# Row-stacked queries for the exact chunks: scores that contract over 64 rows instead of 128 rows with zeros

## The chip, the cores and the metric

The kernel runs on one core of one Trainium2 chip. Its engines are TensorE (PE for its matmuls, PEld for the weight loads that go with them), VectorE (DVE), ScalarE (ACT), GpSimd (POOL) and SyncE (SP, which here only issues transfers). The metric is the device time of one execution in microseconds, the median of three runs.

## The reference, cut to what matters

Two stages are computed, one behind the other. The first is attention over 4 batches, 8 heads, 768 positions and a head size of 64, in which a query sees the first `n_sink` = 4 keys and the `window` = 128 keys up to its own position:

```python
scores = scale * np.matmul(q, k.transpose(0, 1, 3, 2))      # scale = 1 / sqrt(64)
keep = is_sink | in_window
scores = np.where(keep, scores, -1000000000.0)
scores = scores - np.max(scores, axis=-1, keepdims=True)
a = np.exp(scores)
a = a / (np.sum(a, axis=-1, keepdims=True) + 1e-09)
attn_out = np.matmul(a, v).astype(np.float32)
```

The second takes the 3072 rows of that output, 512 wide, through a feed-forward layer of width 2048 with a softplus:

```python
h = x @ w_in
g = np.maximum(h, 0.0) + np.log1p(np.exp(-np.abs(h)))
out = (g @ w_out).astype(np.float32)
```

`w_in` and `w_out` arrive as 64-bit floats; the kernel turns them into pairs of 32-bit numbers on the chip.

## The kernel before, in words

**Tiling.** The 768 positions of a batch are cut into blocks of 128 queries, and two blocks make a chunk of 256 rows (`CT`). There are 12 chunks (`nchunks`), three to a batch. For every head of a chunk `_Attention` runs `load`, `split`, `scores`, `softmax`, `normalise`, `weights_t`, `values` and `out`; for every chunk `_Moe` runs eight steps of `up`, `softplus`, `gate`, `residue` and `down`.

**Two kinds of chunks.** Chunks 2 to 11 compute in pairs of reduced-precision numbers, a high and a low part (`qkh`, `kl`). Their scores put the high parts and the low parts one above the other and contract over 128 rows (lines 230 and 231). The first two chunks (`Ctx.EXACT` = 2) compute scores and values in plain 32-bit floats. There the two heads of a pair lie one above the other in one tile: the keys of head h in rows 0 to 63, those of head h+1 in rows 64 to 127, side by side with the layout array `k0`. The queries come from the array `q0`, which before is 128 rows by two planes of 256 columns: plane 0 holds head h's queries in rows 0 to 63 and zeros below, plane 1 holds zeros above and head h+1's queries in rows 64 to 127. A score of either head is a product over all 128 rows, in which the zeros take the other head out:

```python
            if self.exact:
                q, k = ops
                nc.tensor.matmul(s[:], q[:, j * P : j * P + P], k[:, mv], start=True, stop=True)
```

It stands at line 227 and is made 32 times (2 chunks, 8 heads, 2 blocks). The profile counts two TensorE matmuls and two weight loads for each, 64 in all.

**What sets the order.** The order of the work is written out by hand. A string, `Ctx.START`, names the steps of the first chunks one by one (S is `scores`, T `softmax`, N `normalise`, W `weights_t`, V `values`, O `out`, K `sink`, U `up`, D and E `down`, w a weight transfer, a, c, d and l the four stages that convert a piece of weights); later chunks follow a repeated pattern. It begins with

```python
S0 G4 T0 w w S1 j4 T1 J0 w L8 w w S3 S2 N0 N1 T2 W0 L10 w N2 S4 T3 N3 a w T4 k0 a c K0 a S5 c W1 w w
```

so the two heads of a pair follow each other on TensorE only in S0 S1 and in S3 S2; every other score stands between other matmuls. Engines execute their own instructions in order.

**Transfers.** q0 of the first pair is issued on ACT, as are the small transfer `words` (the sizes, line 77) and all the weights (`w`, line 368); all other loads are issued on SP. Transfers share eight completion counters (named DMAHW0 to DMAHW7 below); a transfer that takes over a counter waits, on the engine that issues it, for the earlier transfer on it.

**The start.** TensorE first runs 16 matmuls on zeros (line 617). `_constants` builds the masks on DVE from `words` (lines 107 to 120). The softmax of a head is, on DVE, a copy of the diagonal (line 243) and a masked maximum (line 249), and on ACT the exponential (line 250).

**The fallback.** `_general`, with `_general_head`, runs only if a flag computed at the end says that the fast path does not hold; none of its lines is in the trace.

Of the kernel before, what the change touches and what calls it, by code (L numbers as in the profile page):

```python
# [11 lines left out]
F32 = mybir.dt.float32  # L12
# [8 lines left out]
B, H, S, D = 4, 8, 768, 64  # L21
DM, DFF = 512, 2048
P = 128
# [4 lines left out]
CT = CH * P  # L28
KC = CH * KW + P
# [93 lines left out]
class _Attention:  # L123
# [42 lines left out]
    def load(self, h):  # L166
        c, nc, chunk, b = self.c, self.c.nc, self.chunk, self.b
        if self.exact:
            if h % 2 == 0:
                early = chunk == 0 and h < 6  # L170
                kp, kt, qp, qt = (c.mp, "gh", c.mp, "gl") if early else (c.lp, "qkh", c.lp, "qk")
                bufs = c.GB if early else 2
                k = kp.tile([P, KC], F32, tag=kt, name=f"k{chunk}_{h}", bufs=bufs)
                nc.sync.dma_start(k[:], c.a["k0"][chunk, h // 2])
                q = qp.tile([P, 2, CT], F32, tag=qt, name=f"q{chunk}_{h}", bufs=bufs)
                (nc.scalar if chunk == h == 0 else nc.sync).dma_start(q[:], c.a["q0"][chunk, h // 2])
                self.heads[h], self.heads[h + 1] = (q[:, 0], k), (q[:, 1], k)
            return
        r = c.lp.tile([P, QK], F32, tag="qk", name=f"qk{chunk}_{h}")
        for half in (r[:D], r[D:]):  # L180
            nc.sync.dma_start(half, c.a["qk"][b, chunk % NCH, h])
        self.heads[h] = r
# [679 lines left out]
def _blocks(w_in, w_out):  # L862

    w_in = w_in.reshape(4, P, FP, 256).transpose(2, 1, 0, 3).reshape(FP, P, WC)
    w_out = w_out.reshape(FP, 2, P, DM).transpose(0, 2, 1, 3).reshape(FP, P, WC)
    w = np.stack([w_in, w_out], axis=1)
    return w.view(np.int64) if w.dtype == np.float64 else w


def _layout(q, k, v, n_sink, window, moe_w_in, moe_w_out):  # L870
    kT = k.transpose(0, 1, 3, 2)
    kA = np.empty((B, H, D, (NB + 1) * KW), k.dtype)
    for j in range(NB + 1):
        i = max(j - 1, 0)
        kA[..., j * KW : j * KW + P] = kT[..., i * P : i * P + P]
        kA[..., j * KW + P : (j + 1) * KW] = kT[..., :NS]
    qT = q.transpose(0, 1, 3, 2)
    qk = np.empty((B, NCH, H, D, QK), k.dtype)
    for n in range(NCH):
        qk[:, n, :, :, :KC] = kA[..., n * CH * KW : n * CH * KW + KC]  # L880
        qk[:, n, :, :, KC:] = qT[..., n * CT : n * CT + CT]
    first = qk[0, : Ctx.EXACT].reshape(Ctx.EXACT, H // 2, 2, D, QK)
    k0 = np.ascontiguousarray(first[..., :KC]).reshape(Ctx.EXACT, H // 2, P, KC)
    q0 = np.zeros((Ctx.EXACT, H // 2, 2, D, 2, CT), k.dtype)
    for e in range(2):
        q0[:, :, e, :, e] = first[:, :, e, :, KC:]
    return {
        "qk": qk,
        "k0": k0,
        "q0": q0.reshape(Ctx.EXACT, H // 2, P, 2, CT),  # L890
        "v": np.ascontiguousarray(v.transpose(0, 2, 1, 3)).reshape(B, NB, P, H * D),
        "vs": np.ascontiguousarray(v[:, :, :NS].reshape(B, 2, G * NS, D).transpose(0, 2, 1, 3)),
        "sizes": np.array([n_sink, window], np.int64).view(np.int32).reshape(1, 4),
        "w": _blocks(moe_w_in, moe_w_out),
    }
# [11 lines left out]
```

## Time and profile before

| | us |
|---|---|
| runs | 733.78, 734.67, 980.27 |
| median | 734.67 |
| profiled execution, its own time | 734.63 |
| span of it, first to last instruction | 732.9 |
| PE busy in the span | 701.2 |
| DVE busy | 566.0 |
| ACT busy | 448.3 |
| POOL busy | 428.9 |

The median is that of all three runs, one of which was much longer. The profiled execution lies 0.04 us below the median, and 1.7 us of its time lie around the span. "Busy" is the time in which an engine had an instruction under way; PE's is modelled and includes waiting inside its pipeline. In the rows below, L227 is line 227 of the kernel, `a<-b,c` names the tile written and those read, `128*128` behind a matmul is the rows and columns of the array that it uses, and `128x264` is the shape of the moving data. A row of the timeline gives start, length, engine, line, operation, tiles, count, and in brackets how long the engine was idle before it and what ended that.

### The profile page before, as it was taken

How to read it: one execution, taken by the hardware profiler on the slowest of the kernel's cores; microseconds unless marked ns; L12 is line 12 of the kernel's file. 1: busy time of each engine (PE TensorE's matmuls, PEld its weight loads, DVE VectorE, ACT ScalarE, POOL GpSimd, SP SyncE). 2: the span in 40 equal slices, each digit the busy share in tenths (PEclk: the TensorE clock that was granted, in tenths of full speed). 3: DMA queues.
4: the chain of work that ended last, by engine and by line, in shares of the span. 5: the costliest groups of instructions: out<-in, count | busy, mean ns of one | idle time of the engine just before them, and what ended most of it. 6: DMA issues, size and time to landing. Idle time of an engine off the chain costs nothing.

```text
span 732.9 us, 13898 instructions
## 1 busy us (share of the span) xinstructions
PE 701.2 (96%) x4505; PEld 624.5 (85%) x4505; DVE 566.0 (77%) x1608; ACT 448.3 (61%) x1098; POOL 428.9 (59%) x773
## 2 busy tenths in 40 slices
PE   5788899999999999999999999999999999999996
PEld 4577789988999999988898999998898998998995
DVE  5899997887887887887987888888887887754321
ACT  4577865756666666765666765765666666644331
POOL 4865476675655765775765665667566576663110
PEclk9899999999999999999999999999999999999998
DMA  9877611411321321312222222221212222100001
GB/s 308 302 249 235 187 40 48 126 47 45 99 68 48 106 67 48 105 55 57 74 74 68 77 77 64 81 70 52 83 54 78 70 74 77 59 12 1 29 1 34
DMA packets 40874, 63.20 MB, mean 86 GB/s; under 512 B 4634, under 2 KB 22362, under 8 KB 40794
## 3 DMA queue, kind: packets, MB, share of 16 engines
q1 hardware_dynamic: 35898, 45.20, 21.1%
q10 hardware_dynamic: 4896, 17.04, 6.9%
q8 instruction: 38, 0.62, 0.4%
q14 instruction: 42, 0.34, 0.2%
HBM read 55.93 MB, written 6.29 MB: 85 GB/s over the span
## 4 chain that ended last, share of the span: by engine, by line
PE 79%; DVE 7%; ACT 6%; POOL 5%; issue 1%; DMA 1%; ACTq 0%; POOLq 0%; DVEq 0%
PE h L459 33%; PE acc L498 10%; PE acc L496 10%; PE acc L497 10%; PE x L333 5%; PE t L297 2%; PE s L230 2%; PE s L231 2%; ACT a L250 2%; PE x L327 2%; DMA q<-q 1%; DVE wt L403 1%; ACT mt L467 1%; ACT mt L468 1%; POOL vs L159 1%
## 5 line engine op out<-in xcount | busy, mean ns | idle before, releaser
L459 PE MATMUL h<-xh,wi 128*128 128x256 f32 x1536 | 255.1, 289 | 0.0
L459 PEld LDWEIGHTS h<-xh,wi 128*128 128x128 f32 x1536 | 212.8, 193 | 1.3 <-issue 0.3
L52 POOL TENSOR_SCALAR gh<-mt 128x512 fp32r<-128x512 f32 x91 | 56.6, 622 | 170.2 <-DVE mt L474 163.6
L459 PE MATMUL h<-xl,wi 128*128 128x256 f32 x768 | 155.3, 284 | 0.0
L496 PE MATMUL acc<-wo,gh 128*128 128x512 f32 x384 | 152.2, 396 | 0.0
L498 PE MATMUL acc<-wo,gl 128*128 128x512 f32 x384 | 151.5, 394 | 0.7 <-DVE gl L56 0.7
L497 PE MATMUL acc<-wo,gh 128*128 128x512 f32 x384 | 151.1, 394 | 0.0
L474 DVE SCALAR_TENSOR_TENSOR mt<-h,mt 128x512 f32<-128x512 f32 x96 | 66.1, 689 | 74.3 <-ACT mt L468 65.2
L466 ACT ACTIVATE mt<-h 128x512 f32<-128x512 f32 x96 | 57.1, 595 | 105.3 <-PE h L459 104.8
L459 PEld LDWEIGHTS h<-xl,wi 128*128 128x128 f32 x768 | 120.4, 193 | 0.0
L250 ACT ACTIVATE a<-a,stats 128x136 f32<-128x136 f32 x192 | 76.2, 397 | 57.3 <-DVE stats L249 57.3
L264 POOL TENSOR_SCALAR a<-a,rc 128x128 f32<-128x128 f32 x180 | 68.1, 390 | 43.3 <-ACT mt L466 28.3
L498 PEld LDWEIGHTS acc<-wo,gl 128*128 128x128 f32 x384 | 72.4, 188 | 17.6 <-DVE gl L56 1.2
L496 PEld LDWEIGHTS acc<-wo,gh 128*128 128x128 f32 x384 | 72.4, 189 | 12.8 <-issue 0.3
L497 PEld LDWEIGHTS acc<-wo,gh 128*128 128x128 f32 x384 | 72.5, 189 | 8.9
L56 DVE TENSOR_TENSOR gl<-mt,gh 128x512 fp32r<-128x512 f32 x96 | 76.8, 800 | 4.1 <-POOL gh L52 4.0
L308 POOL TENSOR_SCALAR_AFFINE_SELECT pt<-tl 128x256 fp32r<-128x256 f32 x80 | 57.9, 724 | 16.9 <-DVE tl L56 16.9
L467 ACT ACTIVATE mt<-mt 128x512 f32<-128x512 f32 x96 | 60.7, 633 | 3.1
L468 ACT ACTIVATE mt<-mt 128x512 f32<-128x512 f32 x96 | 60.7, 632 | 3.1
L48 ACT CAST qkh<-qk 128x656 fp32r<-128x656 f32 x80 | 59.5, 743 | 1.3 <-DMA qk<-qk 1.3
L308 POOL TENSOR_SCALAR_AFFINE_SELECT pt<-th 128x256 fp32r<-128x256 f32 (+1 forms) x96 | 42.9, 446 | 27.9 <-ACT th L48 20.5
L56 DVE TENSOR_TENSOR kl<-qk,qkh 128x400 fp32r<-128x400 f32 x80 | 54.5, 681 | 2.5
(185 smaller groups left out, 1248.4 us busy)
## 6 DMA issues: line engine op xcount, KB each, us to landing
qk<-qk SPq DMA_DIRECT2D x160, 164.0 KB, 3.0
vr<-v SPq DMA_DIRECT2D x32, 192.0 KB, 2.8
out<-o SPq DMA_DIRECT2D x24, 256.0 KB, 2.1
vr<-v SPq DMA_DIRECT2D x16, 128.0 KB, 2.2
q<-q SPq DMA_DIRECT2D x7, 256.0 KB, 4.6
k<-k SPq DMA_DIRECT2D x8, 200.0 KB, 4.2
wi00r<-w ACTq DMA_DIRECT2D x1, 511.8 KB
wi01r<-w ACTq DMA_DIRECT2D x1, 511.8 KB, 5.8
```

The source lines that it names most:

```text
L48: nc.scalar.copy(out, in_)
L56: (nc.vector if eng == "V" else nc.gpsimd).tensor_tensor(out, a, b, ALU.subtract)
L250: nc.scalar.activation(a, a, AF.Exp, bias=nm, scale=-1.0, accum_out=sm[:, j : j + 1])
L264: (nc.vector if eng == "V" else nc.gpsimd).tensor_scalar(a, a, rc[:, j : j + 1], 0.0, ALU.mult, ALU.add)
L308: nc.gpsimd.affine_select(pt[:, e, :, 1], src[:], [[0, CH], [1, P]], ALU.is_ge, 0.0, base=0, channel_multiplier=-1)
L459: nc.tensor.matmul(h[:, j], wt, x, start=k == 0, stop=k >= len(prods) - 2, skip_group_check=True)
L467: nc.scalar.activation(t[:], t[:], AF.Exp, scale=-1.0)
L468: nc.scalar.activation(t[:], t[:], AF.Ln, bias=1.0)
L474: nc.vector.scalar_tensor_tensor(t[:], h[:], 0.0, t[:], ALU.max, ALU.add)
L496: nc.tensor.matmul(acc[:], gh[:, j, q], wh, start=f == 0, stop=False, skip_group_check=True)
L497: nc.tensor.matmul(acc[:], gh[:, j, q], wl, start=False, stop=False, skip_group_check=True)
L498: nc.tensor.matmul(acc[:], gl[:, j, q], wh, start=False, stop=f == 2 * FP - 1, skip_group_check=True)
```

## The change

The queries of a pair are now stacked like the keys: rows 0 to 63 hold head h, rows 64 to 127 head h+1, with one plane of 256 columns and no zeros. Each head's score gets the 64 rows of its own queries and of its own keys. The array `q0` and its eight transfers have half the bytes (128 KB for 256 KB). The code of `scores` is untouched; its matmuls use 64 rows of the array, rows 0 to 63 for even heads and rows 64 to 127 for odd ones.

```diff
@@ load
-                q = qp.tile([P, 2, CT], F32, tag=qt, name=f"q{chunk}_{h}", bufs=bufs)
+                q = qp.tile([P, CT], F32, tag=qt, name=f"q{chunk}_{h}", bufs=bufs)
                 (nc.scalar if chunk == h == 0 else nc.sync).dma_start(q[:], c.a["q0"][chunk, h // 2])
-                self.heads[h], self.heads[h + 1] = (q[:, 0], k), (q[:, 1], k)
+                self.heads[h], self.heads[h + 1] = ((q[e : e + D], k[e : e + D]) for e in (0, D))
@@ _layout
-    q0 = np.zeros((Ctx.EXACT, H // 2, 2, D, 2, CT), k.dtype)
-    for e in range(2):
-        q0[:, :, e, :, e] = first[:, :, e, :, KC:]
+    q0 = np.ascontiguousarray(first[..., KC:]).reshape(Ctx.EXACT, H // 2, P, CT)
...
-        "q0": q0.reshape(Ctx.EXACT, H // 2, P, 2, CT),
+        "q0": q0,
```

On PE the order of the path that runs stays what it was, every score in its old place. The one difference lies in the fallback (its tiles are `gxh` and `gxl`), which does not run:

```order
 L459 MATMUL h_3_13199<-gxh_12429,wi_10068 128x256 x4
-L459 MATMUL h_3_13199<-gxl_12430,wi_10068 128x256 x2
 L496 MATMUL acc_0_13093<-wo_10020,gh_2_13183 128x512
 L497 MATMUL acc_0_13093<-wo_10020,gh_2_13183 128x512
 L496 MATMUL acc_1_13094<-wo_10020,gh_2_13183 128x512
 L497 MATMUL acc_1_13094<-wo_10020,gh_2_13183 128x512
+L459 MATMUL h_3_13199<-gxl_12430,wi_10068 128x256 x2
```

Two matmuls of the fallback moved behind four others. On SP the start keeps its order and its waits, and each q row is half as wide. Behind it, where the first two loads of chunk 2 are issued (`qk_0`, one transfer per half of the rows), the counters are dealt out differently:

```order
-L176 DMA q_6_576<-q 128x512 [waits DMAHW5_49,DMAHW3_49]
+L176 DMA q_6_576<-q 128x256 [waits DMAHW5_49,DMAHW3_49]
 L201 DMA vr_1_588<-v 128x3x128 [waits DMAHW6_49]
 L201 DMA vr_2_804<-v 128x3x128 [waits DMAHW5_49,DMAHW2_49,PE_49]
-L181 DMA qk_0_818<-qk 64x656 [waits DMAHW7_49,DMAHW1_49]
-L181 DMA qk_0_818<-qk 64x656 [waits DMAHW1_49]
+L181 DMA qk_0_818<-qk 64x656 [waits DMAHW6_49,DMAHW1_49]
+L181 DMA qk_0_818<-qk 64x656 [waits DMAHW7_49]
 L181 DMA qk_1_905<-qk 64x656 [waits DMAHW2_49,PE_49]
```

No transfer moved past another; the two halves of `qk_0` wait for other counters than before. On DVE, ACT and POOL the order is the same.

## The prediction

> **What bounds the kernel now.** The page first: the span and the chain that ended last, by engine and by line.
>
> ```profile
> span 732.9 us, 13898 instructions
> PE 79%; DVE 7%; ACT 6%; POOL 5%; issue 1%; DMA 1%; ACTq 0%; POOLq 0%; DVEq 0%
> PE h L459 33%; PE acc L498 10%; PE acc L496 10%; PE acc L497 10%; PE x L333 5%; PE t L297 2%; PE s L230 2%; PE s L231 2%; ACT a L250 2%; PE x L327 2%; DMA q<-q 1%; DVE wt L403 1%; ACT mt L467 1%; ACT mt L468 1%; POOL vs L159 1%
> ```
>
> PE carries four fifths of the chain, almost all in lines that the change leaves alone. Line 227 is not in the list, but the transfer of q is, with 1%. Where each lies is told by the stages (columns: stretch, its length, busy time of PE, PEld, DVE, ACT and POOL, granted clock, DMA share, GB/s) and by line 227's own group.
>
> ```profile
> 15.00:22.00 7.00, 5.50 (x16) 3.67 (x18) 5.30 (x21) 3.99 (x13) 2.36 (x4) 0.52 1.02 408
> 22.00:50.00 28.00, 21.64 (x122) 15.12 (x121) 25.62 (x90) 18.53 (x59) 20.89 (x35) 0.99 0.84 276
> 50.00:90.00 40.00, 35.87 (x201) 29.55 (x201) 38.25 (x83) 30.92 (x66) 22.39 (x24) 0.92 0.73 215
> 90.00:700.00 610.00, 603.13 (x3980) 546.03 (x3979) 481.29 (x1352) 381.70 (x934) 372.03 (x677) 1.00 0.22 64
> ...
> L227 PE MATMUL s<-k,q 128*128 128x264 f32 x64 | 18.9, 427 | 4.6 <-DVE stats L249 2.5 <-issue 1.7 <-PE t L297 0.4
> ```
>
> From 90 us on PE is busy 603 of 610 us: that stretch is PE's own work, none of it changed, and it ends as much earlier or later as it begins. So the whole effect is made before 90 us, where the 64 matmuls of line 227 lie (18.9 us busy) and where PE, DVE and ACT wait for one another. The chain in order of time shows what of it counts (start, length, what).
>
> ```profile
> 0.84 3.54 DMA q<-q
> 4.40 4.63 DMA q<-q
> 9.06 0.34 ACTq L368
> 9.44 0.41 ACT a L250
> ...
> 16.50 0.59 PE ts L281 x2
> 17.09 1.76 PE s L227 x4
> 18.85 0.43 PE t L297 x2
> 19.28 1.76 PE s L227 x4
> ...
> 35.45 1.16 PE s L227 x4
> ```
>
> Up to 9 us the chain is two transfers of q, then ACT's issue of a weight transfer, then ACT's exponential; line 227 is on it at three places, two of them in the stretch at clock 0.52.
>
> **The change part by part. 1. Half the bytes of q.** At the start stand these rows of the timeline, and the transfer rates of the first 10 us in slices of 0.25 us:
>
> ```profile
> 1.27 0.45 ACTq L77 DMA_DIRECT2D words<-sizes  x1
> ...
> 4.67 0.78 PE L617 MATMUL warm<-sk 128*128 128x256 f32 x4
> 5.29 1.95 PE L227 MATMUL s<-k,q 128*128 128x264 f32 x8
> ...
> 5.65 0.17 DVE L107 CAST words_f<-words 128x4 f32<-128x4 int32 x1 [3.25 <-DMA words<-sizes]
> ...
> 7.34 0.49 DVE L243 COPY_PREDICATED s<-diag,s 128x128 f32<-128x128 int32 x2
> ...
> 8.79 0.09 DVE L249 DVE_READ_ACCUMULATOR2_ANT stats<- 128x1 f32 x1
> ...
> 8.98 2.02 PE L227 MATMUL s<-k,q 128*128 128x264 f32 x8 [1.75 <-issue]
> ...
> 9.44 0.41 ACT L250 ACTIVATE a<-a,stats 128x136 f32<-128x136 f32 x1 [0.47 <-DVE stats L249]
> ```
> ```profile
> GB/s 0 0 0 0 0 0 0 102 100 36 145 373 326 408 411 379 277 240 147 38 304 318 337 351 385 405 403 343 274 244 293 360 352 339 369 354 326 343 306 360
> ```
>
> The first q lands at 4.38 us (0.84 + 3.54), but PE is with the warm-up matmuls until 5.3 us, so an earlier q0 starts no score earlier. What it may bring forward is `words`, issued right behind it on ACT: DVE idles 3.25 us for it, builds the masks, and reaches the first softmax copy at 7.34 us. 128 KB fewer at the 326 to 411 GB/s of slices 12 to 16 (2.75 to 4.0 us) (131,072 bytes) are 0.32 to 0.4 us; I take 0.35, since `words` can only be moved after q0 on its own queue. The first two scores end in time for that (the first head half way through the 1.95 us, at 6.27).
>
> The second q of the chain (4.40 to 9.03) holds a counter that ACT's second weight transfer needs. ACT issues at 9.06 and starts head 1's exponential at 9.44, though its input stood at 8.88 (8.79 + 0.09). Of that exponential's delay, 9.44 - 8.88, 0.56 us is waiting for this transfer. By 9.03 three q's (q0, q2, q4) have become 384 KB smaller, 1.1 to 1.2 us at some 340 GB/s, so that wait should go: with the 0.35 before it, head 1 gains up to 0.9 us. But head 2, next on DVE, takes scores that start at 8.98 when head 1's score tiles come free, which is moved by 0.35 alone. What is late next is that pair of scores and DVE's row sums. The start is worth 0.35 to 0.9 us here; I take 0.4, and 0 and 4.1 (half of 3.54 + 4.63, were the chain's first 8.2 us nothing but bytes) as ends. The other five q's land before anything on the chain waits for them; their cover is the whole queue of other work, and without it they would each cost up to 0.4 us.
>
> **2. Scores on 64 rows.** Count and moving columns stay (64 matmuls of 264 columns), so I leave their length at what it was: four take 0.89 us in the row pair 61.21 to 62.10 below. No score of before used 64 rows, so the change between array shapes has to be bounded from other rows. Line 327 (`x`) uses 64 columns, and the PE and PEld rows around it, with line 297's group (277 ns for one), show what a change of shape costs.
>
> ```profile
> 36.45 0.38 PE L297 MATMUL t<-ident,a 128*128 128x128 f32 x2
> 36.76 0.43 PE L327 MATMUL x<-sk,vsf 128*64 128x256 f32 x1
> ...
> 37.67 0.38 PE L333 MATMUL x<-pt,vr 128*64 128x128 f32 x2
> 37.98 1.16 PE L227 MATMUL s<-k,q 128*128 128x264 f32 x4
> 38.98 0.38 PE L297 MATMUL t<-ident,a 128*128 128x128 f32 x2
> ...
> 61.21 1.05 PE L227 MATMUL s<-k,q 128*128 128x264 f32 x4
> 62.10 0.38 PE L297 MATMUL t<-ident,a 128*128 128x128 f32 x2
> ...
> L297 PE MATMUL t<-ident,a 128*128 128x128 f32 x192 | 37.4, 277 | 0.5 <-ACT th L48 0.5
> ```
> ```profile
> 31.32 0.32 PEld L281 LDWEIGHTS ts<-ident,sa 128*32 128x32 f32 x2
> ...
> 36.22 0.36 PEld L297 LDWEIGHTS t<-ident,a 128*128 128x128 f32 x2
> 36.76 0.19 PEld L327 LDWEIGHTS x<-sk,vsf 128*64 128x64 f32 x2 [0.17 <-issue]
> ```
>
> Two 128-column matmuls that together last 0.38 us, one of them 0.27, start 0.11 apart. The second of line 297 thus starts at 36.56, and the next, of another shape, 0.20 later, not 0.11: 0.09 us lost. The weight load shows why: with one shape it runs ahead (36.22 for a matmul at 36.45), across the change it starts with its matmul (36.76 both). From 128\*64 into a score it is the same 0.09 (37.67 + 0.11 to 37.98), and the four scores then take 1.00 us (37.98 to 38.98) instead of 0.89: 0.20 us in all. Going out to a transpose I estimate 0.15, the 0.09 and half of that 0.11.
>
> Against it stands line 281, shape 128\*32, behind a score of 128\*128: its weight load at 31.32 runs 0.22 us ahead of its matmul, which starts at 31.54, so nothing is lost there.
>
> ```profile
> 31.54 0.38 PE L281 MATMUL ts<-ident,sa 128*32 128x128 f32 x2
> ```
>
> A change to 64 rows thus costs between 0 and 0.2 us at full clock; I take the upper end, 64 being nearer to the row of 64 columns. The Trainium skill, "TensorEngine Tiling (Array Packing)", section Tiling Modes, says that changing the tiling mode, not just the tile, drains TensorE: by that rule every change pays and the sum below stands, by the row of 32 columns it would be 734.2. The 64-column rows agree with the page, the 32-column one does not.
>
> By the order on PE, the score blocks bring 20 new changes of shape: 2 for S0 to S3 of chunk 0 together, 1, 2, 1, 2 for its S4 to S7, and 1, 1, 1, 1, 2, 2, 2, 2 in chunk 1 (neighbours of 64 columns had a change already). At 0.2 that is 4.0 us, and the three in the stretch at 0.52 double: 4.6. On the chain lie line 281 to 227 to 297 there (0.4 + 0.3) and the way out behind 35.45 (0.15): 0.85 us. The rest are beside DVE and ACT work (38.25 and 30.92 us busy of the 40 in 50 to 90) and cost nothing while that cover holds.
>
> **3. Counters.** The halves of chunk 2's first load now wait for others.
>
> ```profile
> 70.18 0.74 ACT L48 CAST qkh<-qk 128x656 fp32r<-128x656 f32 x1 [0.85 <-DMA qk<-qk]
> ```
>
> Only this cast waits for them, 0.85 us, and between 0.85 gained and about as much lost is possible; I take 0.
>
> **The sum.** 734.63 (the profiled execution) - 0.4 + 0.85 + 0 = 735.1 us. That execution lies 0.04 us below the median of the runs shown, so it stands for it too. A measurement of this kernel tells about 2% from no change, 720.0 to 749.4 here.
>
> **The rivals.**
> *A, the loads carry through:* everything up to 9 us shortens with the bytes, and more of the 4.1 us arrives. For it: the chain names these transfers. Against it: warm-up, `words` and the score tiles each stand just behind. 730.5 to 733.0; chance 0.13.
> *B, every change of shape counts:* PE has no cover from 15 to 90 us. For it: PE is busy 35.87 of 40 us in 50 to 90. Against it: DVE is busier, and the chain there changes engines often. 734.63 - 0.4 + 4.6 = 738.8, from 736.3 on; it decides as soon as a score waits for nothing but PE. Chance 0.12.
> *C, slower by the clock:* PE's clock falls while less of it is at work; half the rows could be read as less work. The stretch of 7 us at 0.52 loses up to 7 x 0.48 = 3.4 us. One or two more such stretches between 22 and 90 us: 738 to 742; it decides if the clock of 22 to 50 us falls below 0.9. For it: the low stretch goes with an idle time of PE, 3.73 us in the row below, so the clock follows how much PE works. Against it: that is standing still, and no row shows the clock fall under a run of matmuls. Chance 0.06.
>
> ```profile
> 16.50 0.59 PE L281 MATMUL ts<-ident,sa 128*32 128x128 f32 x2 [3.73 <-DVE sa L269]
> ```
>
> *D, the array takes the halves together:* no loss at a change of shape, and the two heads of a pair overlap. Only S0 S1 and S3 S2 stand side by side; of each pair's 1.95 to 2.02 us half could go, about 0.9 on the chain for the second: 734.63 - 0.4 - 0.9 = 733.3, and 734.2 without the overlap. Against it: each head's two blocks share their rows and come one behind the other. Chance 0.18. The Trainium skill, "TensorE: Matmul & The Clock Gate", section Part 3: Packing small matmuls, says that matmuls in different row groups run concurrently; no row here shows 64-row matmuls.
>
> **How the numbers follow.** My forecast, 733.9 to 736.3, has 0.47; A 0.13, B 0.12, C 0.06, D 0.18, and 0.04 lie beyond 2%, in a way that I do not see, half on each side. None of the named cases reaches 2%. From 731.5 to 738.8 all is taken in but the far part of A, most of C and the 0.04.
>
> **What would show it.** Right: line 227 as 64\*128, four of them in 0.9 to 1.0 us; weight loads that no longer run ahead at its edges; `words` at about 5.3 us; head 1's exponential before 9.0; the end 0 to 1.5 us from 732.9. Wrong: edges that lose nothing, a first softmax that stays at 7.3 us, a lower clock in 22 to 90 us, or four scores in clearly less than 0.89 us.

## The result and the profile after

| | before | after |
|---|---|---|
| median of 7 runs, us | 734.65 | 737.37 (735.41 to 739.55) |
| ratio after to before, 95% interval | | 1.0056 (1.0042 to 1.0069) |
| profiled execution, its own time, us | 734.63 | 735.78 |
| span, us | 732.9 | 734.1 |
| PE busy in the span, us | 701.2 | 705.6 |
| mean granted clock of the profiled execution | 0.988 | 0.985 |

Ratios here leave out an execution more than 1.5% above the fastest of its kernel: 980.27 us of before, and 739.88 of after_busy below, with which the ratio of its means would be 0.9992. The ratio of 1.0056 is that of the timing; the two medians of the table divide to 1.0037, and 737.37 over 733.51, the median of 95 later executions of before, is 1.0053.

The kernel became slower by 0.4 to 0.6%, with an interval that leaves out 1. The median is 2.3 us above the forecast of 735.1, above the 733.9 to 736.3 that the forecast itself covers, and inside the wide range of 731.5 to 738.8. The profiled execution is one of the faster ones, 1.6 us below the median, so its trace shows a loss of only 1.2 us.

The page of after, its span, its row of granted clock (40 slices of 18 us, in tenths) and the chain by engine and line:

```profile
span 734.1 us, 13898 instructions
...
PEclk7799999999999999999999999999999999999999
...
PE 80%; DVE 6%; ACT 5%; POOL 5%; issue 2%; DMA 2%; ACTq 0%; SPq 0%; POOLq 0%; DVEq 0%
PE h L459 33%; PE acc L498 10%; PE acc L496 10%; PE acc L497 10%; PE x L333 6%; PE t L297 3%; PE s L230 2%; PE s L231 2%; PE x L327 2%; DMA qk<-qk 2%; ACT a L250 2%; PE s L227 1%; POOL vs L159 1%; POOL pt L308 1%; POOL pt L311 1%
```

The transfer of q has left the list, and line 227 and the transfer of `qk` have come into it. The clock row begins with 77 where that of before has 98: in the first 36 us PE was granted less. The stages of after (stretch, length, busy time of PE, PEld, DVE, ACT and POOL, granted clock, DMA share, GB/s) put it into one of them:

```profile
15.00:22.00 7.00, 5.90 (x14) 3.22 (x15) 4.85 (x19) 4.13 (x12) 2.10 (x3) 0.50 1.01 403
22.00:50.00 28.00, 23.88 (x119) 15.21 (x118) 24.15 (x87) 17.73 (x58) 21.11 (x35) 0.93 0.77 256
50.00:90.00 40.00, 34.62 (x194) 26.94 (x193) 36.83 (x83) 30.04 (x65) 22.43 (x24) 0.96 0.74 212
90.00:700.00 610.00, 603.52 (x3979) 545.67 (x3978) 482.66 (x1354) 383.72 (x937) 371.30 (x677) 1.00 0.22 65
```

From 22 to 50 us the clock is 0.93 (before 0.99), and PE is busy 23.88 us with 119 instructions, where before it needed 21.64 for 122. From 90 us on the busy times agree. The clock record itself gives the edges: before ran at half clock from 15.2 to 22.1 us, after from 8.8 to 25.9. Both had one more short stretch near 50 us, and before a third from 66.4 to 69.8 that after did not have.

The start, from the timeline of after (start, length, engine, line, operation, and in brackets the idle time before it and what ended that):

```profile
5.01 0.17 DVE L107 CAST words_f<-words 128x4 f32<-128x4 int32 x1 [2.60 <-DMA words<-sizes]
5.56 1.17 PE L227 MATMUL s<-k,q 64*128 64x264 f32 x8
...
6.71 0.49 DVE L243 COPY_PREDICATED s<-diag,s 128x128 f32<-128x128 int32 x2
8.34 2.25 PE L227 MATMUL s<-k,q 64*128 64x264 f32 x8 [1.61 <-issue]
8.53 0.41 ACT L250 ACTIVATE a<-a,stats 128x136 f32<-128x136 f32 x1 [0.20 <-DVE stats L249]
9.51 1.33 ACTq L368 DMA_DIRECT2D wo00r<-w  x1
11.24 0.41 ACT L250 ACTIVATE a<-a,stats 128x136 f32<-128x136 f32 x1 [1.81 <-DVE stats L249]
```

Apart from the pair S0 S1 (5.56 for 5.29), everything here is earlier than before: `words` by 0.64 us, the first copy by 0.63, head 1's exponential by 0.91. The same matmuls, matched one for one in the two traces, show what becomes of the lead (after less before): about -0.9 us in S3 S2, -0.41 at the first `ts` (16.10 for 16.50), then +2.1 at 23.7 us, +0.6 at 35.4, +1.4 at 56, -0.6 at 70 (where before has its third half-clock stretch), -0.2 at 81.0, +1.8 at 83.8, and +1.4 to +1.5 from 183 to 707 us. The loss is made between 16.5 and 24 us, at half clock, and PE has caught up by 70. It returns in one step between 81 and 84, at the end of a chain that starts with the load of chunk 2; that load was issued 1.36 us late, when PE was as late (see Counters below).

### The profile page after: what moved, and what is told of

Same layout as the page of the kernel before. It is cut to its first block, busy times and chain, and to the rows that moved or that the text cites. A ratio compares the mean times of both kernels' runs of the same rounds, so it can differ in the third digit from the quotient of the medians.

```text
span 734.1 us, 13898 instructions
## 1 busy us (share of the span) xinstructions
PE 705.6 (96%) x4505; PEld 622.6 (85%) x4505; DVE 565.0 (77%) x1608; ACT 448.8 (61%) x1098; POOL 428.9 (58%) x773
## 4 chain that ended last, share of the span: by engine, by line
PE 80%; DVE 6%; ACT 5%; POOL 5%; issue 2%; DMA 2%; ACTq 0%; SPq 0%; POOLq 0%; DVEq 0%
PE h L459 33%; PE acc L498 10%; PE acc L496 10%; PE acc L497 10%; PE x L333 6%; PE t L297 3%; PE s L230 2%; PE s L231 2%; PE x L327 2%; DMA qk<-qk 2%; ACT a L250 2%; PE s L227 1%; POOL vs L159 1%; POOL pt L308 1%; POOL pt L311 1%
```

## The experiments

All but after are timed in five rounds beside the kernel before, whose median lay between 733.2 and 733.8 us there; the row of after is the result above, with 734.65 beside it. The expectations number the theories in the order in which they were formed; the text names them by content. "Half clock" is the first such stretch behind the start in the clock record of the profiled execution, and "clock" the median over all executions of the mean granted clock.

| kernel | ratio (95%) | median us | clock | half clock, us |
|---|---|---|---|---|
| before (95 executions) | | 733.51 | 0.991 | 15.2 to 22.1 |
| after | 1.0056 (1.0042 to 1.0069) | 737.37 | 0.982 | 8.8 to 25.9 |
| rows_only | 1.0044 (1.0026 to 1.0061) | 736.76 | 0.981 | 8.6 to 25.7 |
| load_only | 1.0003 (0.9989 to 1.0017) | 733.71 | 0.990 | 16.2 to 23.1 |
| c0_rows | 1.0024 (1.0012 to 1.0036) | 735.67 | 0.986 | 11.1 to 24.7 |
| c1_rows | 1.0010 (0.9992 to 1.0029) | 734.66 | 0.988 | 15.8 to 19.3 |
| after_busy | 0.9984 (0.9956 to 1.0012) | 731.59 | 0.994 | none before 46.7 |
| before_busy | 1.0005 (0.9990 to 1.0019) | 733.55 | 0.993 | none before 49.0 |
| after_busy_half | 1.0037 (1.0021 to 1.0052) | 736.99 | 0.986 | 17.8 to 24.7 |
| after_apart | 1.0062 (1.0038 to 1.0086) | 737.15 | 0.985 | 11.8 to 25.5 |
| after_late_w | 1.0048 (1.0035 to 1.0061) | 737.03 | 0.981 | 9.0 to 36.3 |
| after_busy_late_w | 0.9989 (0.9967 to 1.0012) | 732.41 | 0.992 | 24.1 to 27.5 |
| after_busy36 | 0.9987 (0.9965 to 1.0008) | 733.10 | 0.992 | 24.7 to 28.1 |
| c0_busy | 0.9994 (0.9981 to 1.0007) | 733.15 | 0.994 | none before 46.2 |

### rows_only and load_only: the two halves of the change apart

rows_only keeps the old transfers of 256 KB and gives each score the 64 rows that are not zero (against before):

```diff
-                self.heads[h], self.heads[h + 1] = (q[:, 0], k), (q[:, 1], k)
+                self.heads[h], self.heads[h + 1] = ((q[e * D : e * D + D, e], k[e * D : e * D + D]) for e in range(2))
```

> The two-plane queries of before with their zeros and their 256 KB transfers, but the scores read only a head's own 64 rows; the counters are dealt out as in the changed kernel. Theory 1 (the 64-row scores cost the time: they run the first two heads at once, PE stands idle, the clock falls, and the shape changes add to it): 1.0056 of before plus about 0.6 us for the start that is not gained, 1.005 to 1.008, with a stretch at half clock that begins before 12 us and lasts 10 us or more. Rival 2 (the smaller loads shift the start into a worse place): 0.998 to 1.002.

load_only has the new transfers of 128 KB and scores over all 128 rows; it leaves out the separation of the heads, so each score is the sum over both heads of the pair (against after):

```diff
-                self.heads[h], self.heads[h + 1] = ((q[e : e + D], k[e : e + D]) for e in (0, D))
+                self.heads[h], self.heads[h + 1] = (q, k), (q, k)
```

> The stacked queries with 128 KB transfers, but each score contracts over all 128 rows; a head's scores are then the sum of the scores of both heads of its pair, so the separation of the heads is left out. Theory 1: the loads alone gain 0.3 to 1 us, 0.9985 to 0.9998 of before, the first softmax copy at about 6.7 us and the clock as in before (half clock from about 15 to 22 us). Rival 2: 1.003 to 1.006, as slow as the changed kernel.

The 64 rows carry the loss: 1.0044 (a little under the 1.005 expected) with the old transfers and, like after, half clock from 8.6 to 25.7 us. Half the bytes do not bring the gain that was expected: 1.0003, with half clock nearly as before. In the trace of load_only one sees where their gain goes. Rows of ACT, of DVE (the first input of head 2's exponential) and, in the last line, of the chain:

```profile
9.79 2.27 ACTq L368 DMA_DIRECT2D wo00r<-w  x1
10.94 0.08 DVE L249 DVE_READ_ACCUMULATOR2_ANT stats<- 128x1 f32 x1
12.16 0.41 ACT L250 ACTIVATE a<-a,stats 128x136 f32<-128x136 f32 x1 [2.62 <-DVE stats L249]
```
```profile
17.16 0.58 PE ts L281 x2
```

ACT spends 2.27 us issuing the transfer of the weights `wo00r`, which took 0.34 us before (at 10.74) and 1.33 in after (9.51, above). Head 2's exponential stands behind it on ACT and starts at 12.16, though its input stood at 11.02, so the issue held it for 1.1 us; before it starts at 11.64. The first `ts` comes at 17.16, 0.66 us later than before, where PE had been 0.5 us early at S3 S2. Why the same issue takes so different times is not settled: it was longest where it was asked for at 9.79, not at 9.51.

### after_busy and before_busy: PE kept at work on nothing

A new step Z issues matmuls over 128 rows whose results nobody reads, 12 behind S1 and 24 behind S4, in after and, in the same places, in before:

```diff
+    def busy(k):
+        for _ in range(k):
+            c.nc.tensor.matmul(c.warm[:], c.sk[:, :P], c.sk[:], start=True, stop=True)
+    parts["Z"] = (busy, 0)
...
-S0 G4 T0 w w S1 j4 T1 J0 w L8 w w S3 S2 N0 N1 T2 W0 L10 w N2 S4 T3
+S0 G4 T0 w w S1 Z12 j4 T1 J0 w L8 w w S3 S2 N0 N1 T2 W0 L10 w N2 S4 Z24 T3
```

> The changed kernel with matmuls on zeros that nothing reads, 12 behind the first two scores and 24 behind the score of head 4, where PE stands idle. Theory 1 (clock): the long half-clock stretch of the changed kernel (8.8 to 25.9 us) is gone or shorter, and with it most of the loss: 0.996 to 1.001 of before. Rival 3 (shape changes alone, the clock only goes along): no gain against the changed kernel, 1.004 to 1.008.

> The kernel before with the same idle matmuls in the same places, as the counterpart. Theory 1: its shorter half-clock stretch (15.2 to 22.1 us) goes too, 0.994 to 0.999 of before; what the changed kernel with the same matmuls is slower than this one is the price of the shape changes less the gain of the loads, 0 to 2 us. Rival 3: 1.000 to 1.002 and 3 us or more faster than its changed counterpart.

36 matmuls more take away the whole loss of after, 1.0056 to 0.9984, and in its profile the early half-clock stretch with it. In every profile the clock changes only at multiples of 3.41 us from its first rise, which comes at 5.38 us in after and at 5.72 in after_busy. Cut at these edges, the windows of after and then of after_busy are (columns as above; the clock is the third number from the right):

```profile
5.38:8.79 3.41, 1.80 (x13) 1.23 (x14) 3.33 (x22) 1.15 (x5) 1.45 (x3) 1.00 0.98 282
8.79:12.20 3.41, 3.38 (x12) 2.06 (x10) 1.56 (x10) 1.60 (x9) 1.44 (x4) 0.50 0.99 296
12.20:15.61 3.41, 1.13 (x3) 0.33 (x1) 2.54 (x15) 1.59 (x7) 2.32 (x6) 0.50 0.93 287
15.61:19.03 3.42, 2.93 (x8) 1.59 (x8) 1.64 (x5) 3.23 (x9) 0.00 (x0) 0.50 1.02 414
19.03:22.44 3.41, 3.41 (x10) 1.86 (x10) 3.01 (x11) 0.83 (x4) 2.54 (x4) 0.50 1.02 406
22.44:25.85 3.41, 3.41 (x15) 1.98 (x13) 2.15 (x9) 1.25 (x5) 1.19 (x2) 0.50 0.54 215
```
```profile
5.72:9.14 3.42, 3.42 (x26) 2.87 (x27) 3.00 (x22) 1.48 (x7) 1.66 (x4) 1.00 0.88 274
9.14:12.55 3.41, 2.98 (x18) 1.97 (x15) 1.37 (x10) 1.45 (x7) 1.24 (x4) 1.00 0.93 322
12.55:15.96 3.41, 2.22 (x19) 2.01 (x17) 2.58 (x16) 1.58 (x8) 2.33 (x6) 1.00 0.93 317
15.96:19.38 3.42, 3.10 (x13) 1.85 (x14) 2.69 (x8) 2.83 (x9) 0.72 (x2) 1.00 1.03 413
19.38:22.79 3.41, 3.40 (x20) 2.08 (x18) 3.34 (x17) 2.30 (x10) 3.35 (x4) 1.00 1.03 406
```

In after a window with PE busy for 1.80 us comes before the fall at 8.79. The clock then stays down behind a window in which PE is busy for 3.38 us and one in which it is busy throughout (19.03 to 22.44); it rises behind the next, at 25.86. In the window from 19 us on PE has 10 matmuls under way at half clock and 20 at full (none of the idle ones lies there). before_busy missed the gain that was expected of it: in its profile it loses its early half-clock stretch too (none before 49.0 us), but it stays at 1.0005. Rows of PE:

```profile
5.52 3.19 PE L227 MATMUL s<-k,q 128*128 128x264 f32 x8
8.35 1.78 PE L616 MATMUL warm<-sk 128*128 128x256 f32 x12
9.97 1.94 PE L227 MATMUL s<-k,q 128*128 128x264 f32 x8
```

Scores S3 S2 start at 9.97 instead of 8.98, and the first `ts` at 17.43 instead of 16.50; at 23.7 us, behind before's half-clock stretch, PE is 1.3 us ahead. The 0.9 us paid at first are not the price of the idle matmuls alone. In this execution the clock first rose at 8.03 us (before 4.98), so S0 S1 took 3.19 us instead of 1.95 and pushed the idle matmuls back; in before PE stood idle for 1.75 us ahead of S3 S2, about what they take. Why nothing is gained over all 12 executions is open.

### after_busy_half: the same idle matmuls on 64 rows

This is the sharpest question: is it the time for which PE is busy that holds the clock, or how much of the array is? The kernel is after_busy with half the rows in step Z.

```diff
-            c.nc.tensor.matmul(c.warm[:], c.sk[:, :P], c.sk[:], start=True, stop=True)
+            c.nc.tensor.matmul(c.warm[:], c.sk[:D, :P], c.sk[:D], start=True, stop=True)
```

> The changed kernel with the same 12 and 24 idle matmuls in the same places, but each over 64 rows instead of 128. Theory 6 (the clock follows how many rows of the array work, not how long PE is busy): half clock begins by 16 us at the latest and lasts 10 us or more, 1.003 to 1.007 of before, although PE is as busy as with the 128-row ones. Rival 1 (the clock follows PE's busy time alone): full clock to 40 us, 0.996 to 1.001, as with the 128-row ones.

Its time is 1.0037 (1.0021 to 1.0052), apart from after_busy's 0.9984 (0.9956 to 1.0012), with the same number of matmuls at the same places. The windows of after_busy_half, cut at its own clock edges (first rise at 7.59 us):

```profile
11.01:14.42 3.41, 2.98 (x22) 2.86 (x22) 1.74 (x14) 2.04 (x9) 2.34 (x7) 1.00 0.94 318
14.42:17.83 3.41, 2.49 (x16) 1.68 (x15) 2.66 (x11) 2.48 (x9) 0.61 (x2) 1.00 0.97 381
17.83:21.25 3.42, 3.42 (x8) 1.87 (x9) 3.17 (x11) 1.61 (x5) 2.29 (x3) 0.50 1.02 413
```

The clock falls behind a window with PE busy for 2.49 us, 2.17 of it on 64 rows, where after_busy kept it behind 2.22 us, all on 128 rows (12.55 to 15.96). It also kept its clock behind 2.98 us on 64 rows alone (11.01 to 14.42), in which the idle matmuls follow one another closely. That it fell only at 17.8 us, and for 6.8 us, was not as expected (by 16 us and for 10 or more), so in this one profile the idle matmuls of 64 rows held the clock for a while; over 12 executions the clock of 0.986 lies half way between after (0.982) and before (0.991).

### after_apart: without the overlap of a pair

In after the two heads of S0 S1 overlap (1.17 us for the pair, 1.95 before), which makes PE idle sooner; that could have been the reason for the clock instead of the rows. One idle matmul between the heads of each pair ends the overlap:

```diff
-S0 G4 T0 w w S1 j4 T1 J0 w L8 w w S3 S2 N0
+S0 Z1 G4 T0 w w S1 j4 T1 J0 w L8 w w S3 Z1 S2 N0
```

> The changed kernel with one matmul on zeros of 128 rows between the scores of head 0 and 1, and one between those of head 3 and 2, so that the two heads of a pair cannot run at once. Theory 1, by idle time (the overlap makes PE idle and that lowers the clock): the two pairs take 1.9 to 2.3 us again, the half-clock stretch begins at 12 us or later, as in before, and the time falls to 1.001 to 1.004 of before. Rival 6 (the clock falls because 64-row matmuls count as half the work, overlap or not): half clock still from about 9 us, 1.004 to 1.007.

The pairs are one behind the other (rows of PE),

```profile
5.38 1.15 PE L227 MATMUL s<-k,q 64*128 64x264 f32 x4
6.46 0.38 PE L616 MATMUL warm<-sk 128*128 128x256 f32 x1
6.78 1.16 PE L227 MATMUL s<-k,q 64*128 64x264 f32 x4
```

and the time is no better, 1.0062. The overlap is not the cause of the loss, although in this profile the clock fell at 11.8 us, near what the idle-time theory expected, and not at about 9. This run also gives the most direct pair of windows, since its clock rose at the same moment as that of before (4.98 us), so that the steps of both lie at the same times. First before, then after_apart:

```profile
8.40:11.80 3.40, 2.39 (x11) 1.91 (x12) 2.68 (x16) 1.62 (x9) 2.48 (x7) 1.00 1.08 365
11.80:15.20 3.40, 0.97 (x4) 0.49 (x3) 1.80 (x9) 1.88 (x9) 2.32 (x6) 1.00 0.99 365
15.20:18.60 3.40, 2.10 (x6) 1.59 (x7) 2.42 (x11) 3.10 (x10) 0.00 (x0) 0.50 1.04 413
18.60:22.00 3.40, 3.40 (x11) 2.08 (x11) 2.69 (x10) 0.89 (x4) 2.18 (x3) 0.50 1.01 406
22.00:25.50 3.50, 2.72 (x19) 1.88 (x17) 2.83 (x12) 2.53 (x11) 2.85 (x5) 0.99 0.82 290
```
```profile
8.40:11.80 3.40, 2.95 (x12) 1.81 (x12) 1.84 (x14) 0.98 (x6) 1.50 (x5) 1.00 0.90 263
11.80:15.20 3.40, 2.00 (x4) 1.03 (x4) 1.76 (x11) 1.98 (x9) 2.24 (x6) 0.50 0.97 335
...
18.60:22.00 3.40, 3.40 (x9) 1.60 (x8) 2.10 (x6) 0.52 (x2) 1.59 (x3) 0.50 1.00 388
22.00:25.50 3.50, 3.50 (x14) 1.99 (x14) 3.07 (x14) 1.59 (x6) 2.09 (x2) 0.51 0.61 246
```

From 8.4 to 11.8 us before has PE busy 2.39 us, all on 128 rows, and keeps its clock; after_apart has it busy for longer, 2.95 us, 2.3 of it on 64 rows, and loses it. Both windows hold S3 S2, the two transposes behind them and the first matmul of S4; after_apart has one idle matmul besides. From 18.6 to 22.0 both are busy for the whole 3.40 us; before gets its full clock back and after_apart, with 2.7 us of it on 64 rows, stays at half, to rise behind the next window, which is all on 128 rows. The busy time does not order these cases; the rows do.

In the 14 profiles, 275 such windows at full clock end before 90 us, and the clock falls behind 35 of them. PE is busy for up to 2.94 us in those 35, and 82 windows that keep the clock lie below that. With the time on 64 rows counted half, the falls lie at 1.88 us or less, and only 12 windows that keep the clock below that. Counting half is an estimate that orders most windows and not all; how the hardware counts was not shown.

The lengths of the first half-clock stretch fit a step: 6.83 us (before), 17.07 (after), 13.65 (after_apart) and 3.41 (c1_rows) are 2, 5, 4 and 1 times 3.41 us. The Trainium skill, "TensorE: Matmul & The Clock Gate", Part 1, says that the gate goes by how busy TensorE was in a free-running window of 3413 ns. The lengths agree. Busy time as the profile counts it does not decide here: by it after_apart, the busier of the two, should have kept its clock at 11.8 us.

### c0_rows and c1_rows: one chunk at a time

```diff
+                new = (chunk == 0) == True
-                q = qp.tile([P, 2, CT], F32, tag=qt, name=f"q{chunk}_{h}", bufs=bufs)
+                q = qp.tile([P, CT] if new else [P, 2, CT], F32, tag=qt, name=f"q{chunk}_{h}", bufs=bufs)
...
+                if new:
+                    self.heads[h], self.heads[h + 1] = ((q[e : e + D], k[e : e + D]) for e in (0, D))
+                else:
+                    self.heads[h], self.heads[h + 1] = (q[:, 0], k), (q[:, 1], k)
```

In c1_rows the first line reads `== False`.

> Chunk 0 as in the changed kernel, chunk 1 with the two planes and 128 rows as before. Theory 1 (most of the loss is the start: two heads at once, PE idle, half clock from 9 us): 1.002 to 1.006 of before, with the long half-clock stretch. Rival 3 (the changes of shape, of which 8 to 9 lie here and 12 in chunk 1): about 0.4 of the loss, 1.001 to 1.003, and chunk 1 alone the larger part.

> Chunk 1 as in the changed kernel, chunk 0 as before. Theory 1: the clock of the start as before (half clock from about 15 to 22 us), only changes of shape between 26 and 75 us: 0 to 1 us, 0.9995 to 1.0015 of before. Rival 3: 1.002 to 1.005.

Chunk 0, whose scores lie in the early stretch, costs 0.24% and has the long half-clock stretch (11.1 to 24.7 us). Chunk 1 costs 0.10%, with an interval that includes no change at all, and its profile has four short half-clock stretches (15.8, 46.6, 63.6 and 84.1 us). Both have the halved transfers of their chunk as well; together they make 0.34%, beside 0.56% in after and 0.44% in rows_only, within the intervals.

### after_late_w and after_busy_late_w: the issue of the weights out of head 2's way

```diff
-T1 J0 w L8 w w S3 S2 N0 N1 T2 W0
+T1 J0 w L8 w S3 S2 N0 N1 T2 w W0
```

> The changed kernel with the fifth weight transfer (wo00r) issued on ACT behind the exponentials of head 2 instead of ahead of them. Theory 4 (the start's gain is given back because that issue takes 1.3 to 2.3 us while the exponentials of head 2 wait behind it): head 2's first exponential no later than 10.9 us instead of 11.2, and 0.3 to 1.3 us less than the changed kernel, 1.003 to 1.005 of before, since the clock is not touched. Rival 5 (head 2 waits for its scores anyway): no difference, 1.004 to 1.007.

> The changed kernel with the idle matmuls that keep the clock up and with the fifth weight transfer behind the exponentials of head 2. Theories 1 and 4 together: 0.3 to 1.3 us less than with the idle matmuls alone, 0.994 to 0.999 of before. Rival 5: as with the idle matmuls alone, 0.996 to 1.001.

The issue moved, but it had not been what head 2 waited for. Rows of ACT, and of DVE for the input, in after_late_w:

```profile
9.03 1.41 ACTq L368 DMA_DIRECT2D wi11r<-w  x1
10.86 0.08 DVE L249 DVE_READ_ACCUMULATOR2_ANT stats<- 128x1 f32 x1
11.04 0.41 ACT L250 ACTIVATE a<-a,stats 128x136 f32<-128x136 f32 x1 [1.61 <-DVE stats L249]
11.21 0.34 ACTq L368 DMA_DIRECT2D wo00r<-w  x1
```

Head 2's exponential is 0.2 us earlier (11.04 for 11.24), and so is the first `ts` (15.91 for 16.10). But in after, too, the issue was over at 10.84 and the input stood only at 11.14; here ACT is free from 10.44 and the input stands at 10.94. In both the exponential waits for its scores, as rival 5 had it, and these were 0.2 us earlier in a profile whose clock fell at 9.02 instead of 8.79. Of these three traces the issue holds head 2 in load_only alone. In the time nothing of the move is seen: 1.0048, and 0.9989 beside the idle matmuls. In the profile of after_late_w PE stays at half clock until 36.3 us and is up to some 5 us late against before between 28 and 34 us, of which 2.6 us are left at the end. An early 0.2 us is worth nothing beside such a stretch.

### after_busy36 and c0_busy: is there more to gain

Among the 12 executions of after_busy, nine lie at 728.4 to 732.1 us and three at 737.9 to 739.9. Two kernels were to remove these three: one with 36 instead of 24 idle matmuls behind S4, and one that has these 36 and changes chunk 0 alone.

```diff
-N2 S4 Z24 T3
+N2 S4 Z36 T3
```

> The changed kernel with 12 and 36 instead of 12 and 24 idle matmuls, so that the idle 1.5 us that was left behind the 24 is mostly filled. Theory 1: no half-clock stretch before 40 us in any run, and the few slow runs of the version with 24 (738 to 740 us) go: 0.994 to 0.998 of before. Rival 7 (those slow runs have another cause, or the filling now delays the next transposes): as with 24, 0.996 to 1.002.

> 64 rows in chunk 0 alone, chunk 1 with the two planes and 128 rows, and the idle matmuls (12 and 36). Theories 1 and 2 together (clock kept up, and only the changes of shape of chunk 0): 0 to 1 us less than the same with 64 rows in both chunks, 0.993 to 0.998 of before. Rival 7: 0.998 to 1.002.

Both missed the times that theory 1 expected. Neither is faster than after_busy, and after_busy36 keeps the spread (729.8 to 739.0), with a half-clock stretch at 24.7 us in its profile. No version here beats the kernel before: after_busy is lowest with 0.9984, and its interval includes 1.

### All executions together: time and clock

Every execution has its granted clock beside its time, 225 in all over before and the 13 other kernels. With (1 - clock) x 2 x span as the time at half clock, a straight line gives 730.1 us + 0.28 us for each us at half clock, with a correlation of 0.89. With each kernel's own mean taken out, the slope is 0.31, so it is not only a difference between kernels.

| mean granted clock | executions | median us | of these: before | after, rows_only |
|---|---|---|---|---|
| 0.998 and more | 11 | 729.85 | 0 | 0 |
| 0.992 to 0.997 | 83 | 732.82 | 47 | 0 |
| 0.986 to 0.991 | 93 | 734.57 | 48 | 1 |
| 0.980 to 0.985 | 31 | 737.23 | 0 | 10 |
| under 0.980 | 7 | 738.62 | 0 | 3 |

None of 95 executions of before has a clock under 0.986, and 13 of the 14 of after and rows_only have. The three long executions of after_busy have 0.982 and 0.983 and its four shortest 0.999: their spread is the clock again. What decides which execution it hits is not settled. The clock first rises somewhere between 4.97 and 8.03 us in the profiles taken, so the steps fall on the kernel's work differently each time; that this is the reason was not shown.

## Why the prediction was right and wrong

**What bounds the kernel: right.** The whole effect is made before 90 us; behind it PE is busy 603.52 of 610 us (before 603.13), and the lateness at 183 us (1.4) is nearly that at 707 (1.5).

**Half the bytes of q: the mechanism right, the value nothing.** `words` was to come at 5.3 and came at 5.01; head 1's exponential was to come before 9.0 and came at 8.53. The 0.4 us taken for the start is what the first `ts` shows, 0.41. But the price of what moved earlier with it, the issue of `wo00r`, was not in the sum: in load_only it took 2.27 us and held head 2's exponential for 1.1. In after it took 1.33 us and held nothing, since head 2 waited for its scores, as the prediction had said. load_only puts the term at 1.0003 (0.9989 to 1.0017), that is between -0.8 and +1.2 us. Rival A, by which the loads carry through to 730.5 to 733.0, falls with it.

**Scores on 64 rows: the unit price right.** Rows of PE, then of PEld, at a score block in after at full clock:

```profile
45.62 0.40 PE L459 MATMUL h<-xl,wi 128*128 128x256 f32 x2
45.95 1.15 PE L227 MATMUL s<-k,q 64*128 64x264 f32 x4
47.03 0.39 PE L281 MATMUL ts<-ident,sa 128*32 128x128 f32 x2
```
```profile
45.95 0.74 PEld L227 LDWEIGHTS s<-k,q 64*128 64x128 f32 x4
47.03 0.11 PEld L281 LDWEIGHTS ts<-ident,sa 128*32 128x32 f32 x2 [0.34 <-PE s L227]
```

The weight load starts with its matmul (45.95 both), as forecast. The first matmul of the block starts 0.21 us behind the one ahead of it where matmuls of one shape start 0.12 apart, so 0.09 us is lost; within the block the first two start 0.33 apart against 0.22, another 0.11. That is the 0.20 taken for a way in; out of a block it is put at 0.15, and the next matmul comes 0.31 us behind the last instead of 0.22, so 0.09 us is lost there. From its start to the next matmul the block took 1.09 us (45.95 to 47.03) instead of 0.89, a little more than the 0.9 to 1.0 that was to show. Even line 281, whose 32 columns had lost nothing behind a score of 128 rows, now waits (47.03 both). The Trainium skill, "TensorEngine Tiling (Array Packing)", section Tiling Modes, says that a change of mode drains TensorE; at the edges of the 64-row scores the runs agree, at about 0.1 us each.

That most of these changes cost nothing in the end was not shown by itself. Rival B, 738.8 us, has them all count; but after_busy has all of them too and is not slower than before, so they do not come through in full.

**The overlap, rival D, happened and brought nothing.** The prediction held it for unlikely, since each head's blocks share their rows. The two heads' matmuls started 13 ns apart and the pair took 1.17 us instead of 1.95. The Trainium skill, "TensorE: Matmul & The Clock Gate", Part 3: Packing small matmuls, says that matmuls in different row groups run concurrently, and the trace agrees. Yet after_apart, without the overlap, has the same time (737.15 and 737.37): what follows S0 S1 and S3 S2 waits for DVE and ACT.

**Counters: not shown apart.** The cast that waits for them came later,

```profile
72.36 0.74 ACT L48 CAST qkh<-qk 128x656 fp32r<-128x656 f32 x1 [2.05 <-DMA qk<-qk]
```

2.05 us waited for 0.85, and the chain names the transfer (rows of the chain):

```profile
59.99 0.53 SPq L181
60.57 11.72 DMA qk<-qk
```

SP issues at 59.99, 1.36 us later than before (58.63); the load of `vr_2` ahead of it waits for PE, which was 1.4 us late there. From that issue to the cast lie 11.55 us in before and 12.37 in after, but 10.65 in after_apart and 10.90 in after_busy, which differ from after on PE alone. So this is mostly the lateness of PE carried on, and nothing here points to the new counters; no run tries them alone.

**The failed step: the clock, put at nothing in the sum and at 0.06 as rival C.** The prediction set four scores at their old length and let only the edges count, and it argued that the clock falls when PE stands still and that "no row shows the clock fall under a run of matmuls". It does fall under one: after_apart has PE busy 2.95 of 3.40 us from 8.4 to 11.8, more than before, and falls at 11.8. In after_apart and in after the clock also stays at half behind a window that is busy throughout but mostly on 64 rows (18.6 to 22.0 and 19.0 to 22.4), and rises behind the next one, which is all or mostly on 128. So by these windows half the rows are read as less work, as rival C put it. In after itself the fall at 8.8 us comes behind a window in which PE was idle for nearly half, with S0 S1 done in 1.17 us instead of 1.95; there idle time and half rows act together. With the pair apart, in after_apart, PE was busy for 2.96 us in the window up to 8.38 and the clock held, so the idle time had its part in that first fall. Of the "what would show it wrong" list this came true: 0.93 instead of 0.99 from 22 to 50 us (and four scores in clearly less than 0.89 us, for S0 S1 alone, where eight took 1.17). Rival C's size was off: it needs the clock under 0.9 there and gives 738 to 742. It counted up to 0.48 us for each us at half clock, and the runs show 0.28, perhaps because part of PE's work there lies beside DVE and ACT. After's median clock is 0.009 lower than before's: 0.009 x 2 x 734 = 13 us more at half clock, at 0.28 us are 3.7 us. The gap between 737.37 and before's 733.51 is 3.9; against the 734.65 of its own session it is 2.7.

**The number.** 737.37 lies in the wide range, but in the part above 736.3 that was there for rival B, with another mechanism. That the range holds the result is luck: the sum had neither the clock nor its price.

## What to carry to other kernels

Where a kernel's start leaves TensorE little work, the zeros in a 128-row matmul can be worth more than they cost: matmuls over half the rows took as long here and let the clock fall. Before trading rows for bytes, look at the granted clock around the place, and if it is near an edge, price each us that may go to half clock (0.28 us here). And when a step is brought forward, follow what it issues: a transfer asked for while others are outstanding can hold the issuing engine, and the compute behind it, for longer than the step gained (1.1 us held against 0.5 gained in load_only).

## What the runs showed of the hardware

- Matmuls over 64 of 128 rows hold the clock less well than matmuls over 128 rows, even where PE is busy for longer (2.95 us of 3.4 fell, 2.39 did not; in after 36 idle matmuls of 128 rows give 0.9984, of 64 rows 1.0037). Idle matmuls whose results nobody reads hold it up (no half clock before 46.7 us in after_busy, 49.0 in before_busy).
- Between the first rise and the end of the kernel, the half-clock stretches of the 14 profiles were 3.41 us long or a multiple of it, and began at times that differ from one profile to the next.
- Two plain 32-bit products in rows 0 to 63 and 64 to 127 start 13 ns apart without anything being asked for; eight took 1.17 us instead of 1.95.
- One issue of a weight transfer on ACT took 0.34 us (asked for at 10.74), and 1.41, 1.33 or 2.27 us asked for at 9.03, 9.51 and 9.79, with other transfers under way; what sets the length was not found.
